# Query weights under four scales instead of one, with group 0's weight sums moved to GpSimd

## Chip, cores and metric

One NeuronCore of a Trainium2 chip runs one program. The metric is the device time of a run in microseconds. A core has a matrix engine (TensorE, PE in the profile, with its weight loads as PEld), VectorE (DVE), ScalarE (ACT), GpSimd (POOL) and a queue that issues DMAs (SyncE, SP). Each works through its own list of instructions in order, and they wait for each other by semaphores.

## The reference

Two blocks read the same normalised input, and the output joins them:

```
xn = layernorm(x)                          # 2048 x 640
q  = (xn @ wq), 32 heads of 192            # wq is 640 x 6144
p  = softmax(q k^T / sqrt(192)), the last 512 keys of the cache
s  = (p v, heads joined) @ wo              # wo is 6144 x 640
h  = sigmoid(xn @ w_gate) * (xn @ w_up)    # 2048 x 1536
g  = silu(h @ w_down)
out = x + s * g
```

All inputs and the output are bf16.

## The kernel before

**Opening** (lines 272 to 559). The 2048 rows of x stand in four tiles of 512 (s = 0 to 3). For each tile the kernel makes xn, turns it by DMA, and runs twelve steps f. A step multiplies a 128-wide slice of w_gate and of w_up (ten matmuls, L493) into a pair of PSUM banks; four pairs are used in turn. ACT takes the sigmoid (L498), and DVE multiplies the two halves into hT_sb (L499). After a tile, four DMAs (store_h, L479) write hT to DRAM (h_d); it is read again much later. Two hT buffers take turns.

Beside these steps the opening prepares the attention. It multiplies q with Strassen-like sums: a product of 2 x 2 blocks in seven half-size products, so that both xn and wq need sums and differences of their blocks in fp16. sum_x (L448) makes those of xn on DVE, six per half pi of the rows; it needs a copy of the odd tile with its partition halves exchanged, which swap (L440) makes by four DMAs on SP. Wq comes in eight groups of 768 columns (two pairs of heads each), each in five chunks c of its rows: load_raw (L223) loads a chunk, scale_raw (L238) scales it to fp16 on ACT or DVE, copy_w (L248) and sum_w (L256) write the sums.

The scale must be known first. It is a power of two near the largest sum of magnitudes, so the whole of wq is read once more: sixteen slices of 128 x 1920 (scan_load, L196) are reduced, thirteen by ACT's Abs with an accumulator (scan_abs, L295) and three by DVE (scan_fold, L200). set_scale (L208) reduces the sums to one number per partition and turns it by a DMA (mx_row); set_scale2 (L216) takes the maximum over it and writes w_up (for the weights) and w_down (for K, scale_k, L164, so that the scores come out the same). One scale serves all groups. Group 0's sums are made in the opening, by ACT (copies) and DVE (subtractions) at the steps in scale_at and sum_at; group 1's raw chunks are scaled at the steps in raw_at.

**Attention** (from L561). Sixteen runs r = (pi, g): a half of the rows and a group. Before run 0 its queries are made alone, in eleven slots (query_slots, L592; the list at L751): a slot is ten matmuls (L584) into PSUM banks, copied by `saved` (L603 on ACT) to a tile qp and added by DVE (L622) into qT. Between the slots second_w (L265) makes two chunks of group 1 on GpSimd and loads the next. In a run there are 16 score steps k (stage_s, L667: six matmuls, L678, and ACT's exponential, L682, into E; two pairs of banks in turn), with the slots for the next run's queries between them (q_after, L758), and then eight steps of p times v (stage_pv, L684: L692 on PE, L698 and L699 on DVE). phase_s (L833) hangs other work on steps k: K and V loads, sums of magnitudes over v and wo on ACT (abs_v, abs_wo). The sums of a later group's weights run at the end of a run (weights, L760) on ACT and GpSimd.

**End.** After the attention come the products with w_down and wo (L1000).

**What sets the order.** The schedule is written by hand: each engine's list has the order of the program text, and SP's and POOL's lists include their DMAs. Memory is laid out by pools. The opening's pools are closed before the attention's are opened, and those take the same addresses from the bottom up; the first instruction that writes into a reused address waits for everything that still reads or writes it. In the opening the pools stand in the order wB (w_gate, w_up, and four scan slices "more"), bwork, bone, hpool (the two hT), xpool, xin_pool, xt_pool. In the attention: arm_pool, small, qT_pool, qp_pool, e_pool, ost_pool, oT_pool. One tile, mid, serves both.

The copy out of a slot's product, and the place of the pool that the opening's hT takes:

```
            else:
                t = qp_pool.tile([P, 512], F32, name="qp")[:]
            copy(t, b, act)
            return t
...
        bone = bctx.enter_context(tc.tile_pool(name="bone", bufs=1))
        hpool = bctx.enter_context(tc.tile_pool(name="hpool", bufs=2))
        xpool = bctx.enter_context(tc.tile_pool(name="xpool", bufs=4))
```

Of the kernel before, what the change touches and what calls it, by code (L numbers as in the profile page):

```python
# [9 lines left out]
ALU = mybir.AluOpType  # L10
# [7 lines left out]
def kernel(  # L18
# [88 lines left out]
    def part(tile_, at, shape, dtype):  # L107
        n = 1
        for m in shape:
            n *= m  # L110
        v = tile_[:, at:at + n]
        if dtype != BF16:
            v = v.bitcast(dtype)
        names = "abc"[:len(shape)]
        if len(shape) == 1:
            return v
        return v.rearrange(
            f"p ({' '.join(names)}) -> p {' '.join(names)}", **{c: m for c, m in zip(names[1:], shape[1:])}
        )
# [10 lines left out]
    w_sc = const.tile([P, 17], F32, name="w_sc")  # L130
    mx_h, h_up, h_down, mx_w, wd_up, wd_down, g_scale = (w_sc[:, i:i + 1] for i in range(10, 17))
# [6 lines left out]
    mx, w_up, w_down, mx_o, o_up, o_down, mx_v, v_up, v_down, descale = (w_sc[:, i:i + 1] for i in range(10))  # L138
# [8 lines left out]
    wq_n = A_wq.rearrange("(p c) n -> p (c n)", p=P)  # L147
# [16 lines left out]
    def scale_k(key):  # L164
        k_sb = k_pool.tile([P, KC * PC, 2, HF], BF16, name="k_sb")
        for i in range(2):
            nc.vector.tensor_scalar(k_sb[:, :, i, :], kraw_of[key][:, i, :, :], w_down, None, op0=ALU.mult)
        k_of[key] = k_sb
# [21 lines left out]
    NPC = 16  # L190
    NSC = NG * NCD * GC // NPC
    assert NSC <= NW // 4
    scan_bufs = [part(mid, (2 * n + 1) * NCD * 512, (NSC,), BF16) for n in (1, 2, 3)]
    scan_bufs += [part(mid, NX + i * NW // 4, (NSC,), BF16) for i in range(4)]

    def scan_load(i, eng):  # L196
        scan_t[i] = scan_bufs[i % len(scan_bufs)]
        eng.dma_start(scan_t[i], wq_n[:, i * NSC:(i + 1) * NSC])

    def scan_fold(wm, i, first):  # L200

        v = scan_t[i]
        bits = (wm[:] if first else v).bitcast(I32)
        nc.vector.tensor_single_scalar(bits, v.bitcast(I32), 0x7FFF7FFF, op=ALU.bitwise_and)
        if not first:
            nc.vector.tensor_tensor(wm[:], wm[:], v, ALU.max)
# [9 lines left out]
    def set_scale2(mx=mx, up=w_up, down=w_down, k=1.0 / 4096):  # L216
        nc.vector.tensor_reduce(mx, mx_row[:, 0, :], axis=mybir.AxisListType.X, op=ALU.max)
        nc.vector.tensor_scalar(down, mx, k, None, op0=ALU.mult)
        nc.vector.reciprocal(up, down)  # L219
# [3 lines left out]
    def load_raw(g, c, eng):  # L223
        raw = raws[raw_next[0] % 3]
        raw_next[0] += 1
        for r in (LO, HI):
            eng.dma_start(raw[r], wq_r[:, c, :, g * GC:(g + 1) * GC])  # L227
        raw_t[g, c] = raw
# [9 lines left out]
    def scale_raw(g, c, on_act=True):  # L238
        raw = raw_t[g, c]
        if on_act:  # L240
            nc.scalar.activation(raw.bitcast(F16), raw, AF.Copy, scale=w_up)  # L241
        else:
            nc.vector.tensor_scalar(raw.bitcast(F16), raw, w_up, None, op0=ALU.mult)
# [4 lines left out]
    def copy_w(g, c, copy):  # L248
        for k, r in enumerate((LO, HI)):
            copy(sums_w(g, c, r, 0), part_w(g, c, r, k, 0))  # L250
# [13 lines left out]

    def second_w(c):  # L265

        copy_w(1, c, nc.gpsimd.tensor_copy)
        sum_w(1, c, nc.gpsimd.tensor_tensor, nc.gpsimd.tensor_copy)
        load_raw(1 + (c + 3) // NCD, (c + 3) % NCD, nc.gpsimd)


    with ExitStack() as bctx:
# [3 lines left out]
        hpool = bctx.enter_context(tc.tile_pool(name="hpool", bufs=2))  # L276
        xpool = bctx.enter_context(tc.tile_pool(name="xpool", bufs=4))
        xin_pool = bctx.enter_context(tc.tile_pool(name="xin_pool", bufs=1))
        xt_pool = bctx.enter_context(tc.tile_pool(name="xt_pool", bufs=1))

# [9 lines left out]
        wmax = bone.tile([P, NSC], BF16, name="wmax")  # L290
        scans = bone.tile([P, 14], F32, name="scans")
        scan_out = bone.tile([P, 3 * D], BF16, name="scan_out")
        x_tiles = {}

        def scan_abs(i, col):  # L295
            nc.scalar.activation(scan_t[i], scan_t[i], AF.Abs, accum_out=scans[:, col:col + 1])
# [40 lines left out]
        more = wB.tile([P, 4, NSC], BF16, name="more")  # L337
        scan_bufs.extend(more[:, i, :] for i in range(4))
        for i in range(4):
            scan_load(i, nc.sync)  # L340
# [107 lines left out]
        def sum_x(pi, k, x_sw):  # L448
# [12 lines left out]
            elif k == 5:  # L461
                tt(xb[HI], ev[HI], xb[HI], ALU.subtract)

        sums = {(1, 4): (0, 4), (1, 10): (0, 0), (1, 11): (0, 1), (2, 7): (0, 2), (2, 9): (0, 3), (2, 11): (0, 5),
                (3, 2): (1, 0), (3, 3): (1, 1), (3, 5): (1, 2), (3, 8): (1, 3), (3, 9): (1, 4), (3, 10): (1, 5)}
        folds = {(1, 7): 10, (1, 8): 11, (1, 9): 12}
        scan_act = {(0, 7): 0, (0, 8): 1, (0, 9): 2, (0, 10): 3, (1, 1): 4, (1, 2): 5, (1, 3): 6, (1, 7): 7, (1, 8): 8,
                    (1, 10): 9, (2, 0): 13, (2, 1): 14, (2, 2): 15}
        scan_loads = {(0, 8): (4, 5, 6), (0, 9): (7,), (0, 10): (8,), (0, 11): (9,), (1, 1): (10, 11, 12),
                      (1, 7): (13, 14, 15)}  # L470
        abs_at = [(0, 3), (0, 4), (2, 4), (3, 4)]
        scale_at = {(2, 7): 0, (2, 9): 1, (3, 0): 2, (3, 3): 3, (3, 6): 4}
        sum_at = {(2, 8): 0, (2, 10): 1, (3, 1): 2, (3, 4): 3, (3, 7): 4}
        raw_at = {(3, 8): 0, (3, 10): 1}
# [6 lines left out]
        for s in range(NST):  # L481
            hT_sb = hpool.tile([P, TQ, NF, P], BF16, name="hT_sb")
            pi = s // 2
            if s % 2 == 1:
                sw = swap(pi)
            for f in range(NF):
# [31 lines left out]
                if (s, f) in folds:  # L518
                    scan_fold(wmax, folds[s, f], folds[s, f] == 10)
                if (s, f) in scan_act:  # L520
                    scan_abs(scan_act[s, f], 1 + list(scan_act).index((s, f)))
# [4 lines left out]
                for i in scan_loads.get((s, f), ()):  # L526
                    scan_load(i, nc.sync)
                if (s, f) == (2, 1):
                    nc.vector.tensor_reduce(scans[:, 0:1], wmax[:], axis=mybir.AxisListType.X, op=ALU.max)
                    for c in range(3):  # L530
                        load_raw(0, c, nc.sync)
                elif (s, f) == (2, 3):
                    set_scale(scans[:])
                elif (s, f) == (2, 6):
                    set_scale2()
                if (s, f) in ((1, 1), (2, 4), (3, 1)):
                    store_h(s - 1, h_last)
                if (s, f) in scale_at:
                    scale_w(0, scale_at[s, f])
                if (s, f) in raw_at:  # L540
                    scale_raw(1, raw_at[s, f])
                if (s, f) in sum_at:
                    c = sum_at[s, f]
                    sum_w(0, c)
                    load_raw((c + 3) // NCD, (c + 3) % NCD, nc.sync if s == 2 else nc.gpsimd)
                if (s, f) == (2, 8):
                    load_k((0, 0))
                if s == 3:
                    if f in (0, 7):
                        scale_k((0, f // 7))  # L550
                    elif f in (3, 9):
                        turn_k((0, f // 9))
                    if f == 0:
                        load_k((0, 1), nc.gpsimd)
                    elif f == 6:
                        for hp in range(G):
                            load_v(0, hp, nc.sync)
# [8 lines left out]
    wo_in = [part(arm, NW + n * NWC * D, (NWC, D), BF16) for n in range(4)]  # L566
    v_abs = part(arm, NW + 2 * NO, (KC, DH), BF16), part(mid, NX, (KC, DH), BF16)
    assert 3 * NO + KC * DH <= NW + NR
# [182 lines left out]
    for n, k in enumerate((0, 1, 7, 2, 3, 8, 4, 5, 9, 6, 10)):  # L751
        slots[k]()
        if n == 1:
            nc.scalar.activation(mx, w_up, AF.Exp, scale=0.0)
        if n < 2:
            second_w(n)
    scale_s = {0: 2, 3: 3, 15: 4}
# [75 lines left out]
    def phase_s(r, pi, g, k, q_list, pv_list):  # L833
# [24 lines left out]
        if pi == 1 and g < NG - 1 and k in (1, 3, 4, 5):  # L858
            abs_v(g, (1, 3, 4, 5).index(k))
        if r in (2, 10) and k == 7:  # L860
            set_scale(*((hw_sum[:, 0:4], mx_h) if r == 2 else (hw_sum[:, 4:8], mx_w)))
# [39 lines left out]
    for r, (pi, g) in enumerate(runs):  # L901
# [23 lines left out]
        for k, (q, x) in enumerate(pv_list):  # L925
            stage_pv(q, *x)
            if r == last - 1 and k == 1:
                set_scale(v_sum[:], mx_v)
            if k in (5, 7):
                store_o(2)  # L930
            if pi == 0 and 1 <= g < 5 and k == 6:
                w = wo_in[3 * g % 4]
                nc.scalar.activation(w, w, AF.Abs, accum_out=hw_sum[:, 3 + g:4 + g])
            if pi == 0 and 1 <= g < NG - 1 and k in (2, 4):
                weights(g + 1, 2 + k // 2)
            if pi == 1 and g + 2 < NG and k in (1, 3, 5):
                weights(g + 2, k // 2)
# [254 lines left out]
```

## Time and profile before

| | |
|---|---|
| median of 3 runs | 888.09 us (887.02 to 888.36) |
| the profiled execution's own time | 887.34 us |
| its span in the profile | 885.6 us |
| mean granted clock of TensorE | 0.993 |
| busy: PE, DVE, ACT, POOL | 868.2, 679.7, 629.3, 211.8 us |
| PE busy, 14 to 116 us | 99.32 of 102 us |
| DVE and ACT busy, 14 to 116 us | 74.38 and 80.97 us |
| one run of the attention (172.4 to 205.1 us) | 32.7 us, PE busy throughout |

The span is what the hardware profiler saw of the program; the time of the execution lies 1.74 us above it. The page gives, per engine, the busy time; slices of a fortieth of the span with tenths of busy time; the clock that TensorE was granted; the chain of waits that ended last; and groups of instructions by line with their mean duration. A window's row has the busy time of each engine in it. A timeline's row has start, duration, engine, line, operation, tiles, and in brackets the idle time before it with what ended it.

### The profile page before, as it was taken

How to read it: one execution, taken by the hardware profiler on the slowest of the kernel's cores; microseconds unless marked ns; L12 is line 12 of the kernel's file. 1: busy time of each engine (PE TensorE's matmuls, PEld its weight loads, DVE VectorE, ACT ScalarE, POOL GpSimd, SP SyncE). 2: the span in 40 equal slices, each digit the busy share in tenths (PEclk: the TensorE clock that was granted, in tenths of full speed). 3: DMA queues.
4: the chain of work that ended last, by engine and by line, in shares of the span. 5: the costliest groups of instructions: out<-in, count | busy, mean ns of one | idle time of the engine just before them, and what ended most of it. 6: DMA issues, size and time to landing. Idle time of an engine off the chain costs nothing.

```text
span 885.6 us, 19009 instructions
## 1 busy us (share of the span) xinstructions
PE 868.2 (98%) x7548; PEld 568.9 (64%) x7557; DVE 679.7 (77%) x1153; ACT 629.3 (71%) x784; POOL 211.8 (24%) x293
## 2 busy tenths in 40 slices
PE   9999959999999999999999999999999999999998
PEld 5444425756766765765775775775777777777775
DVE  6587757777777777777777877787888788879997
ACT  6867746488888888888888786747555666866662
POOL 0000175206415415425424423300000110000000
PEclk9999979999999999999999999999999999999999
DMA  9997881689789789799779769799695976776741
GB/s 279 270 292 159 237 197 37 95 228 211 151 218 213 154 217 219 137 214 236 127 196 225 140 153 203 187 224 259 138 286 176 304 238 208 236 267 212 220 141 38
DMA packets 257177, 175.88 MB, mean 199 GB/s; under 512 B 162432, under 2 KB 239872, under 8 KB 257088
## 3 DMA queue, kind: packets, MB, share of 16 engines
q1 hardware_dynamic: 251040, 155.59, 68.7%
q0 software_dynamic: 6048, 19.08, 10.9%
q8 instruction: 59, 0.97, 0.5%
q14 instruction: 30, 0.25, 0.1%
HBM read 101.71 MB, written 36.70 MB: 156 GB/s over the span
## 4 chain that ended last, share of the span: by engine, by line
PE 84%; issue 1%; DVE 1%; ACT 0%; ACTq 0%; DVEq 0%
PE ps_all L1000 25%; PE ps_all L584 20%; PE ps_all L692 20%; PE ps_all L678 19%; DVE arm L984 0%; DVE arm L1055 0%; DVE arm L1053 0%; DVE qT L622 0%; ACT qp L603 0%; ACTq L603 0%; DVEq L622 0%; DVEq L1053 0%
## 5 line engine op out<-in xcount | busy, mean ns | idle before, releaser
L682 ACT ACTIVATE E<-ps_all 128x1024 bf16<-128x1024 f32 x256 | 251.2, 1022 | 113.5 <-PE ps_all L678 112.8
L678 PE MATMUL ps_all<-qT,kT 64*128 64x512 bf16 x1536 | 198.1, 376 | 0.0
L692 PEld LDWEIGHTS <-E 128*128 128x128 bf16 x2048 | 169.7, 98 | 8.1 <-issue 8.1
L692 PE MATMUL ps_all<-v_sb,E 128*128 128x193 bf16 x2048 | 174.0, 247 | 0.0
L622 DVE TENSOR_TENSOR qT<-ps_all,qp 128x512 bf16<-128x512 f32 x174 | 115.5, 687 | 54.5 <-PE ps_all L584 36.8
L1000 PEld LDWEIGHTS <-mid 128*128 128x128 f16 x1236 | 120.3, 98 | 46.0
L605 DVE COPY qp<-ps_all 128x512 f32<-128x512 f32 x150 | 100.5, 687 | 46.5 <-PE ps_all L584 46.5
L678 PEld LDWEIGHTS <-kT 64*128 64x128 bf16 x1536 | 84.9, 94 | 79.4 <-issue 4.4
L699 DVE TENSOR_TENSOR o_st<-ps_all,rden 128x768 bf16<-128x768 f32 x128 | 122.5, 957 | 4.6 <-DVE rden L698 0.2
L584 PE MATMUL ps_all<-mid 64*128 64x512 f16 (+1 forms) x840 | 109.8, 383 | 8.9 <-ACT qp L603 4.5
L584 PE MATMUL ps_all<-mid,arm 64*128 64x512 f16 (+1 forms) x840 | 105.6, 376 | 0.0
L584 PEld LDWEIGHTS <-mid 64*128 64x128 f16 x840 | 49.9, 95 | 55.3 <-issue 15.2
L584 PEld LDWEIGHTS <-arm 64*128 64x128 f16 x840 | 47.1, 94 | 44.6 <-issue 0.2
L1000 PE MATMUL ps_all<-arm,mid 128*128 128x320 f16 x480 | 70.4, 299 | 0.0
L813 ACT ACTIVATE mid<-mid,w_sc 128x1536 f16<-128x1536 bf16 (+1 forms) x43 | 61.4, 1451 | 0.0
L241 ACT ACTIVATE mid<-mid,w_sc 128x1536 f16<-128x1536 bf16 x37 | 58.2, 1572 | 2.5 <-DVE w_sc L219 1.9
L1000 PE MATMUL ps_all<-op,mid 128*128 128x320 f16 (+1 forms) x408 | 58.1, 295 | 0.0
L499 DVE TENSOR_TENSOR hT_sb<-ps_all,sig_sb 128x512 bf16<-128x512 f32 x48 | 32.8, 684 | 26.3 <-ACT sig_sb L498 17.0
L1000 PE MATMUL ps_all<-mid 128*128 128x320 f16 x348 | 49.9, 299 | 0.0
L259 POOL TENSOR_TENSOR arm<-mid 128x384 f16<-128x384 f16 x20 | 19.3, 963 | 114.5 <-ACT mid L241 113.5
L227 POOL DMA_DIRECT2D mid<-in_A_wq_dram x70 | 41.7, 598 | 13.4 <-DVE mid L263 13.4
L698 DVE RECIPROCAL rden<-ps_all 128x4 f32<-128x4 f32 x128 | 23.3, 182 | 27.7 <-PE ps_all L692 26.1
(189 smaller groups left out, 1055.6 us busy)
## 6 DMA issues: line engine op xcount, KB each, us to landing
oT_d<-oT SPq DMA_DIRECT2D x64, 384.0 KB, 5.5
mid<-oT_d SPq DMA_DIRECT2D x46, 384.0 KB, 4.1
mid<-in_A_wq_dram POOLq DMA_DIRECT2D x70, 192.0 KB, 6.5
arm<-in_A_wo_dram SPq DMA_DIRECT2D x16, 480.0 KB, 5.8
h_d<-hT_sb SPq DMA_DIRECT2D x16, 384.0 KB, 5.7
v_sb<-in_A_v_cache_dram SPq DMA_DIRECT2D x32, 192.0 KB, 6.1
mid<-in_A_wq_dram SPq DMA_DIRECT2D x12, 480.0 KB, 7.4
kraw<-in_A_k_cache_dram SPq DMA_DIRECT2D x30, 192.0 KB, 3.2
```

Source lines behind the costliest of these rows:

```text
L227: eng.dma_start(raw[r], wq_r[:, c, :, g * GC:(g + 1) * GC])
L241: nc.scalar.activation(raw.bitcast(F16), raw, AF.Copy, scale=w_up)
L499: nc.vector.tensor_tensor(hT_sb[:, :, f, :], *(v.rearrange("p (q n) -> p q n", q=TQ) for v in (gu[:, 1, :], sig_sb[:])), ALU.mult,)
L584: nc.tensor.matmul(ps_all[:, b, :], lhsT=w(r, c), rhs=x[r, c, :], start=(first and k == 0), stop=(k == len(cs) - 1), skip_group_check=True,)
L605: nc.vector.tensor_copy(dst, part(b))
L622: nc.vector.tensor_tensor(q_out(i, u, pp), part(b), t, ALU.add)
L678: nc.tensor.matmul(ps[:, b, :], lhsT=kT[h, c * PC + j, :], rhs=qT_t[r][i, j][h, pp, :], start=(j == 0), stop=(j == PC - 1),)
L682: nc.scalar.activation(E_t[r, i, pp][:, c, :, :], ps, AF.Exp, scale=scale_qk)
L692: nc.tensor.matmul(o_ps[:, q // 2, q % 2, 0:DH + 1], lhsT=E[:, c, h, q * P:(q + 1) * P], rhs=vt[:, c, 0:DH + 1], start=(c == 0), stop=(c = ...
L699: nc.vector.tensor_tensor(o_st[:, :, h * DH:(h + 1) * DH].rearrange("p (b i) d -> p b i d", b=2), o_ps[:, :, :, 0:DH], rden[:].to_broadcas ...
L813: eng.activation(t, t.bitcast(BF16), AF.Copy, scale=up)
L1000: nc.tensor.matmul(ps_all[:, b, d0:d1], lhsT=a[:, c, :], rhs=w[:, c, d0:d1], start=(start and c == 0), stop=(c == nk - 1), skip_group_chec ...
```

## The change

**Scales.** wq is scanned in twenty slices of 128 x 1536 instead of sixteen of 128 x 1920: five slices (one per c) for each set of two groups. There are four sets, each with a pair of w_ups and w_downs. Set 0 is scanned in the opening, by ACT alone, at steps 7 to 11 of tile 0; its scale is set at steps (1, 0) and (1, 2). Sets 1 to 3 are scanned by ACT in the attention: slices 5 to 9 after run 0's scores, 10 and 11 among run 0's scores (k = 4 and 10), 12 to 19 one per run at the end of runs 1 to 8. Their scales are set in runs 1, 4 and 9, with the same operations and one more mx_row DMA each. Six slices are loaded by SP between the slots before run 0, the others a run ahead. DVE's three folds and its reduce are gone.

**Group 0's sums.** pool_w makes copies and subtractions of a chunk on GpSimd, where ACT and DVE did; chunks 0 to 4 of group 0 are scaled by ACT at the steps (1, 3), (1, 7), (1, 10), (2, 2), (2, 8), and two of group 1 at (3, 1), (3, 4). All raw loads of the opening go over SP, and so do those of K for pair (0, 1).

**Buffers.** hpool moves behind xt_pool; "more" and the 3840-byte wmax are gone. In the built program the tiles that matter lie at these byte addresses of a partition:

| | before | after |
|---|---|---|
| hT_sb, two | 74848 to 99424 | 91520 to 116096 |
| x_odd, two, and x_sw | 114784 to 135264 | 71040 to 91520 |
| qp, four | 76288 to 84480 | 76384 to 84576 |
| E, four | 84480 to 117248 | 84576 to 117344 |

**Steps.** Some of sum_x, abs_up and store_h stand at other steps. TensorE's instructions are the same in number and order.

The diff, cut to its core:

```diff
-        hpool = bctx.enter_context(tc.tile_pool(name="hpool", bufs=2))
         xpool = bctx.enter_context(tc.tile_pool(name="xpool", bufs=4))
         xin_pool = bctx.enter_context(tc.tile_pool(name="xin_pool", bufs=1))
         xt_pool = bctx.enter_context(tc.tile_pool(name="xt_pool", bufs=1))
+        hpool = bctx.enter_context(tc.tile_pool(name="hpool", bufs=2))
...
+    NSC = 2 * GC
+    NPC = NSET * NCD
+    def scan_load(i, buf):
+        scan_t[i] = buf[:, 0:NSC]
+        n, c = divmod(i, NCD)
+        nc.sync.dma_start(scan_t[i], wq_n[:, c, n * NSC:(n + 1) * NSC])
+    def scan_abs(i):
+        nc.scalar.activation(scan_t[i], scan_t[i], AF.Abs, accum_out=scan_sum[:, i:i + 1])
+    def set_scan(n):
+        set_scale(scan_sum[:, n * NCD:(n + 1) * NCD])
...
+    def pool_w(g, c):
+        copy_w(g, c, nc.gpsimd.tensor_copy)
+        sum_w(g, c, nc.gpsimd.tensor_tensor, nc.gpsimd.tensor_copy)
...
-        more = wB.tile([P, 4, NSC], BF16, name="more")
-        scan_bufs.extend(more[:, i, :] for i in range(4))
-        for i in range(4):
-            scan_load(i, nc.sync)
+        for i, x in enumerate((XA[1], XB[1], XC[1], x_even[1], x_odds[1])):
+            x = x.rearrange("p c n -> p (c n)")
+            scan_load(i, x if x.dtype == BF16 else x.bitcast(BF16))
...
-        sums = {(1, 4): (0, 4), (1, 10): (0, 0), (1, 11): (0, 1), (2, 7): (0, 2), (2, 9): (0, 3), (2, 11): (0, 5),
-                (3, 2): (1, 0), (3, 3): (1, 1), (3, 5): (1, 2), (3, 8): (1, 3), (3, 9): (1, 4), (3, 10): (1, 5)}
-        folds = {(1, 7): 10, (1, 8): 11, (1, 9): 12}
-        abs_at = [(0, 3), (0, 4), (2, 4), (3, 4)]
-        scale_at = {(2, 7): 0, (2, 9): 1, (3, 0): 2, (3, 3): 3, (3, 6): 4}
-        sum_at = {(2, 8): 0, (2, 10): 1, (3, 1): 2, (3, 4): 3, (3, 7): 4}
-        raw_at = {(3, 8): 0, (3, 10): 1}
+        sums = {(1, 4): (0, 4), (1, 9): (0, 0), (1, 11): (0, 1), (2, 7): (0, 2), (2, 9): (0, 3), (2, 11): (0, 5),
+                (3, 2): (1, 0), (3, 3): (1, 1), (3, 5): (1, 2), (3, 7): (1, 3), (3, 8): (1, 4), (3, 10): (1, 5)}
+        abs_at = [(1, 8), (2, 9), (3, 2), (3, 6)]
+        raw_loads = {(0, 9): (0, 0), (0, 10): (0, 1), (0, 11): (0, 2), (1, 11): (0, 3), (2, 3): (0, 4),
+                     (2, 9): (1, 0), (2, 11): (1, 1), (3, 5): (1, 2)}
+        raw_at = {(1, 3): (0, 0), (1, 7): (0, 1), (1, 10): (0, 2), (2, 2): (0, 3), (2, 8): (0, 4),
+                  (3, 1): (1, 0), (3, 4): (1, 1)}
...
+                if s == 0 and 7 <= f:
+                    scan_abs(f - 7)
+                if (s, f) in raw_loads:
+                    load_raw(*raw_loads[s, f], nc.sync)
+                if (s, f) == (1, 0):
+                    set_scan(0)
+                    sw = swap(0)
+                elif (s, f) == (1, 2):
+                    set_scale2()
+                if (s, f) in raw_at:
+                    scale_raw(*raw_at[s, f])
+                    if raw_at[s, f][0] == 0:
+                        pool_w(*raw_at[s, f])
...
         if n < 2:
             second_w(n)
+        elif n == 4:
+            for i in range(6):
+                scan_load(NCD + i, scan_bufs[i])
+    scans_s = {(0, 4): 10, (0, 10): 11}
+    scans_pv = {(0, 0): 5, (0, 1): 6, (0, 2): 7, (0, 4): 8, (0, 6): 9, (1, 7): 12, (2, 7): 13, (3, 7): 14}
+    scans_pv.update({(4 + n, 7): 15 + n for n in range(NCD)})
+    scans_load = {(0, 6): (11, 5), (1, 4): (12, 4), (2, 4): (13, 5), (3, 4): (14, 4)}
+    scans_load.update({(4 + n, 4): (15 + n, 5 - n % 2) for n in range(NCD)})
+    sets = {(1, 1): 1, (4, 1): 2, (9, 1): 3}
+    sets2 = {(1, 8): 1, (4, 9): 2, (9, 8): 3}
```

## The prediction

> **What bounds the kernel now.** I read the page first. TensorE (PE) is busy for almost the whole span, so time can only go where it is not; the slices show one such place.
>
> ```profile
> PE 868.2 (98%) x7548; PEld 568.9 (64%) x7557; DVE 679.7 (77%) x1153; ACT 629.3 (71%) x784; POOL 211.8 (24%) x293
> ...
> PE   9999959999999999999999999999999999999998
> ...
> PEclk9999979999999999999999999999999999999999
> ```
>
> Slice 6 (110.7 to 132.8 us) is half empty and its granted clock is 0.7. Next I asked for busy times by window around it:
>
> ```profile
> 96.00:116.00 20.00, 18.06 (x81) 7.82 (x81) 15.73 (x29) 15.23 (x22) 4.77 (x8) 1.00 1.07 265
> 116.00:120.00 4.00, 2.89 (x20) 1.08 (x20) 3.94 (x5) 3.51 (x5) 3.20 (x3) 1.00 1.02 197
> 120.00:125.00 5.00, 2.22 (x9) 0.65 (x9) 2.67 (x3) 0.00 (x0) 4.70 (x5) 0.77 0.28 112
> 125.00:130.00 5.00, 0.53 (x2) 0.10 (x1) 0.41 (x1) 1.08 (x2) 4.67 (x8) 0.50 1.01 296
> 130.00:135.00 5.00, 4.80 (x33) 2.14 (x33) 1.56 (x3) 4.32 (x8) 3.05 (x5) 0.71 0.63 142
> 135.00:150.00 15.00, 15.00 (x141) 8.76 (x139) 12.14 (x20) 8.82 (x12) 7.69 (x12) 1.00 0.10 27
> ```
>
> The columns are the window, its length, then busy time of PE, PEld, DVE, ACT, POOL, then clock, DMA share, GB/s. PE is idle 1.94 us before 116 and about 8.6 us from 116 to 135. In windows of 20 us from 135 to 875 PE is busy all the time: later work has no hole to fill and must only not make one. The timeline says who is late at the join of opening and attention:
>
> ```profile
> 122.04 0.69 DVE L499 TENSOR_TENSOR hT_sb<-ps_all,sig_sb 128x512 bf16<-128x512 f32 x1
> 122.76 2.32 SPq L479 DMA_DIRECT2D h_d<-hT_sb  x4
> 122.78 2.29 PE L584 MATMUL ps_all<-mid 64*128 64x512 bf16 x9 [2.85 <-DVE hT_sb L499]
> ...
> 128.90 1.08 ACT L603 ACTIVATE qp<-ps_all 128x512 f32<-128x512 f32 x2 [9.39 <-issue]
> 129.55 0.58 PE L584 MATMUL ps_all<-mid 64*128 64x512 f16 x1 [4.47 <-ACT qp L603]
> ```
>
> PE finishes the opening's last matmul at 115.3, but DVE makes the last hT only by 122.73: its queue is backed up with sums. Four stores of that hT to DRAM follow. ACT's first copy out of the query products (qp) waits 9.39 us; the timeline calls it "issue", but the view of the tile h_d names this copy as its one waiter, 9.4 us. In the built program qp lies over an hT buffer. The chain of waits, in order of time, agrees:
>
> ```profile
> 119.51 9.23 issue
> ...
> 130.33 9.58 PE ps_all L584 x74
> 139.91 1.29 PE ps_all L678 x12
> 141.20 1.08 PE ps_all L584 x10
> ```
>
> The first score matmul starts at 139.91, that is 24.67 us after the first query matmul (115.24). One query slot (10 matmuls) takes 1.08 us when nothing waits.
>
> **The change, part by part.**
>
> *Order of buffers.* In the built program of the changed kernel qp lies over x_odd and x_sw, hT only under the E tiles. ACT's first qp copy then waits for the four swap DMAs of the fourth tile, long landed, and for its product. The h_d wait moves to the first exponential.
>
> *Sums of group 0 on GpSimd.* DVE loses five chunks of four subtractions (0.35 + 0.36 + 0.36 + 0.36 = 1.43 us), three folds (0.65 + 1.16 us, the first 0.65) and a reduce of 2.10 us: 7.2 + 4.3 + 2.1 = 13.6 us. ACT loses 15 copies (0.52 us each, 7.8 us). I recount DVE's last steps with T the end of the opening's matmuls and 2.16 us per step f (ten matmuls 0.216 us apart). f7: hT 0.69, sum 1.49, K scaling 0.87 end at T-5.3. f8: hT and sum end at T-3.1. f9: hT at T-2.4. f10: hT and sum at T+0.3. f11: last hT at T+1.0, where it was T+7.4. Its PSUM bank is first needed by the third query slot, at T+2.2, so all three stalls on L499 (0.52, 0.90, 2.85 us) go.
>
> *The join anew.* Eleven slots at 1.08 us are 11.9 us. What is late next: ACT holds a table load (1.28 us) and 0.6 us copies, and its last copy before the third s3 slot ends near T+8.6, when PE is at T+8.6. DVE's additions for the last slot end near T+10.9, PE wants them at T+10.8. So 12.4 us, of 24.67: I take 12.2 us gained. The ends: 11.9 us (12.8 gained), and the eight later slots' own rate in this run, 9.58 / 8 x 11 = 13.2 us (11.5 gained); this row is partly under a clock of 0.71, and gaps up to 0.93 us at 106.85 left it at 1.00, so I lean to the first.
>
> *Opening.* PE idles 102 - 99.32 = 2.68 us between 14 and 116. The largest part, around 104 to 109, comes after DVE waited 1.67 us for x_sw, whose swap (SP, 94.52) stood behind a weight load that waited for DVE's L263. That load now waits for GpSimd, done earlier, so the swap starts near 90. Gain 0 to 2.7 us; I take 1.5. The first slice scan shrinks: 5 x 1.48 us on ACT in the opening for 13 x 1.81 us (1.48 us is interpolated from 128x768, 0.82 us start to start, and 128x1920, 1.81 us). POOL takes five chunks of some 5.5 us (126.49 to 132.0), or 8.6 beside busy DVE (116.66 to 125.25); the last starts near 82 and is wanted at T+3, so it is hidden by 20 us. Two new waits stand in queues. SP's loads of raw weights wait for GpSimd; the last ahead of the swap needs chunk 3, done by 78, and the swap is ready near 90. DVE's set_scale2 comes two steps (4.3 us) after the transpose that it reads, whose landing took 2.2 to 5.2 us: DVE may wait some 1 us near 43, and the hT behind it has three steps, 6.5 us, before PE wants its bank. I cost both at nothing.
> A row that speaks against this part: POOL's L259 and L260 took 2.02 and 2.04 us beside DVE's L460 and L462, for 0.91 alone, and L460 took 1.62 for 1.48. By the rows DVE pays 0.14 us for each of 12 sums, 1.7 us, inside its slack. The Trainium skill ("SBUF — State Buffer", section "SBUF: two separate sides") says why: the two engines share a port pair under an exclusive lock, held for an instruction. By its rule each of 12 DVE sums could wait out a GpSimd operation of 0.91 us, 10.9 us in all; the rows show the loss on POOL's side. DVE is idle 102 - 74.4 = 27.6 us there and 13.6 us are freed, so both fit; it is a rival below.
>
> *Fifteen scans in the attention.* 15 x 1.48 = 22.2 us on ACT, beside PE's work. Five follow run 0's exponentials: 7.4 us inside ACT's idle 10.55 us. Eight of the rest stand at the end of a run's PV part:
>
> ```profile
> 205.95 1.94 ACT L682 ACTIVATE E<-ps_all 128x1024 bf16<-128x1024 f32 x2 [2.54 <-PE ps_all L678]
> ```
>
> ACT is idle 2.54 us there (3.32 us at 238.79, after the next run), so 1.48 us fits. Scan 10 (k=4 of run 0) pushes exponential 5 by 0.8 us, and the pause before score 7 takes it up. Scan 11 (k=10) stands where ACT has none: exponentials 11 and 12 start at 157.44 right behind a qp copy. Moved by 1.48 us, 12 ends at 160.9, and score 14, which needs its banks, would have started at 159.44: 1.4 us lost. Bounds 0 (if exponential 11 slips ahead of need) and 3.3 us (if its load, issued behind scan 10's end, takes the longest h_d landing of 9.8 us).
>
> *Three more scales.* Each puts four DVE operations (219.33 to 220.02, 0.69 us) at k=1 and three (81.41 to 82.08) later. DVE idles 0.24 to 0.44 us per slot and catches up in two; I take 0, bound 3 x 0.69 = 2.1 us. Loads of 0.39 MB a run go over SP where nothing urgent follows.
>
> **Sum**, against this execution's own 887.34 us (span 885.6): -12.2 - 1.5 + 1.4 = -12.3, so 875.0. The median of the runs shown, 888.09, lies 0.75 above it: **875.8 us**. Ends: -12.8 - 2.7 = -15.5 (872.6) and -11.5 + 3.3 + 2.1 = -6.1 (882.0).
>
> **Rivals.**
> 1. *The store wait only moves to the first exponential.* It is wanted at T+13.1; the stores leave at T+1.0 and took 6.0 us (122.76 to 128.74). Against: 6 us of room. For: six scan slices (2.4 MB) come behind them, another h_d issue row lasted 6.17 us, and the longest landing was 9.8: 1.0 + 6.2 + 9.8 = T+17.0, 3.9 us lost: 879.7. Chance 0.18.
> 2. *GpSimd holds DVE up in the opening* (the lock above): then 1.5 us is not won and as much as today's 2.7 us comes on top: 880.0. Against: 41 us of DVE slack. Chance 0.05.
> 3. *ACT becomes the bound, slower.* If each scan delays the exponentials by its full length and PE waits, 22.2 us are paid for 13.7 won: 896.6. It decides where ACT's idle time at a run's end is under 1.48 us; the rows say 2.54. Chance 0.05.
> 4. *The join does not shorten*, because some other buffer or weight of the attention lands when hT did (weights of group 1, K): 888. Against: GpSimd's second group starts with the last hT and is first needed a run later. Chance 0.03.
> 5. *More than forecast*, under 872.6: 0.05.
>
> The forecast has 0.64. The range **872 to 882** takes in rivals 1 and 2. A run of this kernel tells 0.2% (1.8 us) from no change: faster 0.92, same 0.03, slower 0.05.
>
> **What would show it.** Right: first score matmul near 126; no idle ACT before the first qp copy over 1 us; clock 1.00 in every window from 116 to 135; last hT within 2 us of the last opening matmul; PE idle of about 1.4 us in run 0, before score 13 or 14, nowhere later. Wrong: the first exponential waiting on h_d; exponentials late at a run's start; PE idle after 160.

## The result, and the profile after

The changed kernel takes 877.85 us (median of 4 runs, 877.32 to 878.37), the kernel before beside it 887.56 us (886.62 to 888.36). The ratio is 0.9891, with a 95% interval of 0.9874 to 0.9908. The profiled execution's span is 876.1 us, where it was 885.6. The forecast was 875.8, so the direction and the place were right, and 2 us are missing.

First the page of the kernel after: busy times, then slices of PE and of its clock.

```profile
PE 865.4 (99%) x7557; PEld 570.9 (65%) x7557; DVE 674.9 (77%) x1148; ACT 628.5 (72%) x783; POOL 234.8 (27%) x320
...
PE   9999999999998999999999999999999999999998
...
PEclk9999999999999999999999999999999999999999
```

The half-empty slice 6 has gone, and with it the dip of the clock. A smaller dent has appeared at slice 13 (262.8 to 284.7 us). The windows at the join (window, length, busy PE, PEld, DVE, ACT, POOL, then clock, DMA share, GB/s):

```profile
120.00:125.00 5.00, 5.00 (x48) 2.35 (x46) 4.67 (x8) 2.22 (x5) 4.52 (x7) 1.00 1.01 330
125.00:130.00 5.00, 5.00 (x50) 2.62 (x46) 4.11 (x6) 3.82 (x4) 4.73 (x7) 1.00 1.04 251
130.00:135.00 5.00, 5.00 (x49) 2.64 (x47) 4.60 (x7) 4.29 (x5) 4.68 (x8) 1.00 0.30 61
```

PE is busy throughout and the clock is 1.00, where it was busy 2.22, 0.53 and 4.80 us at 0.77, 0.50 and 0.71. The timeline of the kernel after says why:

```profile
112.63 0.69 DVE L490 TENSOR_TENSOR hT_sb<-ps_all,sig_sb 128x512 bf16<-128x512 f32 x1
...
113.66 0.60 ACT L588 ACTIVATE qp<-ps_all 128x512 f32<-128x512 f32 x1 [1.66 <-PE ps_all L569]
...
124.83 1.94 ACT L667 ACTIVATE E<-ps_all 128x1024 bf16<-128x1024 f32 x2 [0.25 <-PE ps_all L663]
```

The last hT ends 0.9 us after the opening's last matmul (T = 112.44; for the profiles of before, T is the start of the first query matmul, which lies within 0.1 us of it). The first copy to qp waits for PE alone. The first exponential, which now lies behind the stores of hT, waits 0.25 us, for its own matmuls. The chain of waits (start, us, what; in order of time) gives the join and what follows:

```profile
112.44 11.70 PE ps_all L569 x105
124.14 1.29 PE ps_all L663 x12
...
141.72 1.46 ACT arm L202 x2
143.18 1.84 ACT E L667 x2
```

The join takes 11.70 us, which was 24.67. The first score comes at 124.14, 15.77 us earlier than before. Of that, run 0 gives back 1.22 us: scan 11 (L202) stands in the chain ahead of two exponentials. Run by run the first scores then keep a distance of 14.6 us to those of before until run 4. That run lasts 38.14 us, where it lasted 32.85, and 9.4 us are left to the end. The timeline of run 4 in the kernel after (SPq is what SP issues; the brackets hold the idle time before a row and what ended it):

```profile
259.24 5.81 SPq L690 DMA_TRANSPOSE oT<-o_st  x1
260.54 0.61 DVE L212 CAST mx_b<-w_sc 128x128 bf16<-128x128 f32 x1
...
265.78 3.44 SPq L184 DMA_DIRECT2D v_sb<-in_A_v_cache_dram  x4
...
272.27 1.31 SPq L213 DMA_TRANSPOSE mx_row<-mx_b  x1
276.58 0.29 DVE L216 TENSOR_REDUCE w_sc<-mx_row 128x1 f32<-128x128 bf16 x1 [4.43 <-DMA mx_row<-mx_b]
277.90 1.26 PE L569 MATMUL ps_all<-mid 64*128 64x512 f16 x10 [3.49 <-DVE qp L590]
```

This is the third set's scale. Its input is ready at 261.15, but SP sends the transpose only at 272.27, behind a transpose of outputs, their stores and the v loads. It lands at 276.57. DVE has reached set_scale2 4.43 us earlier and waits there, with the copies of the query products behind it; PE waits 3.49 us for those. The windows around it:

```profile
275.00:280.00 5.00, 2.10 (x16) 1.05 (x17) 1.95 (x6) 0.74 (x1) 0.00 (x0) 0.91 0.58 157
280.00:285.00 5.00, 5.00 (x39) 3.00 (x36) 2.68 (x6) 3.59 (x4) 0.00 (x0) 0.75 0.24 79
```

Around the pause the granted clock is 0.91 and 0.75, so that 3.49 us without work cost 5.29 us.

### The profile page after: what moved, and what is told of

It is laid out like the page before. It is cut to its first block, busy times and chain, and to the rows that moved or that the text cites. A ratio compares the mean times of both kernels' runs of the same rounds, so it can differ in the third digit from the quotient of the medians.

```text
span 876.1 us, 19052 instructions
## 1 busy us (share of the span) xinstructions
PE 865.4 (99%) x7557; PEld 570.9 (65%) x7557; DVE 674.9 (77%) x1148; ACT 628.5 (72%) x783; POOL 234.8 (27%) x320
## 4 chain that ended last, share of the span: by engine, by line
PE 94%; ACT 2%; DMA 1%; DVE 1%; SPq 1%; issue 0%; DVEq 0%; ACTq 0%
PE ps_all L1007 25%; PE ps_all L677 20%; PE ps_all L569 19%; PE ps_all L663 18%; PE ps_all L484 11%; ACT E L667 1%; PE ps_all L387 1%; ACT arm L722 1%; DMA mx_row<-mx_b 0%; DMA kraw<-in_A_k_cache_dram 0%; SPq L697 0%; DMA x_sb<-in_A_x_dram 0%; DVE arm L991 0%; DVE arm L1062 0%; DVE arm L1060 0%
## 5 line engine op out<-in xcount | busy, mean ns | idle before, releaser
L569 PE MATMUL ps_all<-mid 64*128 64x512 f16 (+1 forms) x840 | 106.8, 377 | 3.5 <-DVE qp L590 3.5
L490 DVE TENSOR_TENSOR hT_sb<-ps_all,sig_sb 128x512 bf16<-128x512 f32 x48 | 32.8, 686 | 28.3 <-PE ps_all L484 20.7
L489 ACT ACTIVATE sig_sb<-ps_all 128x512 bf16<-128x512 f32 x48 | 28.4, 596 | 35.3 <-PE ps_all L484 33.9
L258 POOL TENSOR_TENSOR mid<-mid 128x384 f16<-128x384 f16 x20 | 18.2, 909 | 118.9 <-ACT mid L240 117.9
```

The lines of the kernel that those rows point to most:

```text
L258: tt(TB, part_w(g, c, a, 1, 1), part_w(g, c, a, 0, 1), ALU.subtract)
L569: nc.tensor.matmul(ps_all[:, b, :], lhsT=w(r, c), rhs=x[r, c, :], start=(first and k == 0), stop=(k == len(cs) - 1), skip_group_check=True,)
```

## Experiments

The theory after this reading has four parts. The join was two waits in a row, DVE's lateness and the stores under qp, and each half of the change removes one. The opening gained because the last tile's swap goes out earlier. Scan 11 costs 1.2 us. The third set costs 5.3 us because its transpose stands behind other work on SP. The rivals are named with each run. Every time is a median; ratios are to the kernel before, run beside it (medians 887.5 to 888.3 us).

### The join: order of buffers alone, and all but the order

In the kernel before, only the pool was moved:

```diff
-        hpool = bctx.enter_context(tc.tile_pool(name="hpool", bufs=2))
         xpool = bctx.enter_context(tc.tile_pool(name="xpool", bufs=4))
         xin_pool = bctx.enter_context(tc.tile_pool(name="xin_pool", bufs=1))
         xt_pool = bctx.enter_context(tc.tile_pool(name="xt_pool", bufs=1))
+        hpool = bctx.enter_context(tc.tile_pool(name="hpool", bufs=2))
```

> The kernel before, with only the pool of hT moved behind xt_pool: DVE is as late as before (last hT 7.4 us after the opening's last matmul, T), but the first copy to qp no longer waits for the stores of hT. Theory (two waits stand one behind the other, and each part of the change removes one): third slot waits for DVE until about T+8; the second of the two spare copies, whose tile now lies under the last hT, waits for the stores until about T+13.5; four or five slots are left then; first score near T+19 instead of T+24.7, so 5 to 6 us less than before: about 882. Rival a (the stores' wait was the whole join): first score near T+13, 12 us less, about 876. Rival b (DVE's lateness was the whole): no difference, 887.6.

880.87 us, ratio 0.993 (0.9905 to 0.9954). The opening ends at 113.25 in this profile, and the first score comes at 132.78, T+19.5. The timeline of this kernel:

```profile
120.04 0.69 DVE L499 TENSOR_TENSOR hT_sb<-ps_all,sig_sb 128x512 bf16<-128x512 f32 x1
...
120.79 10.53 PE L584 MATMUL ps_all<-mid 64*128 64x512 bf16 x72 [2.84 <-DVE hT_sb L499]
```

DVE is as late as expected, at T+7.5 (120.73), and PE waits for it as before. After that PE does not stop again, so the wait that I expected at the spare copies is not there. The rest is the clock: the chain's 84 matmuls, which take 9.1 us at 0.108 us each, take 11.99, at a clock of 0.50 in the window from 120 to 125. Of the 7.2 us between this span (878.4) and that of before (885.6), 5.1 lie in the join, as the theory said; 2.0 lie in the opening, which ended earlier here.

The reverse, in the changed kernel with the pool put back behind bone:

> The changed kernel, with the pool of hT back behind bone, so that qp lies over the last hT again: DVE is on time (last hT at T+0.9), but the first copy to qp waits for the stores of hT, which leave at T+1 and took some 6 us. Theory: that copy starts near T+7 instead of T+1.2 and PE, two slots ahead, loses 5 to 6 us: first score near T+17.3, about 883.5. Rival a (order is all of the join): 12 us lost, 890. Rival b (order is nothing once DVE is on time): 877.9.

884.32 us, ratio 0.9961 (0.9948 to 0.9974), where 883.5 was expected. DVE is on time (last hT at T+1.0, with T = 112.50), and ACT's first copy waits:

```profile
118.96 1.08 ACT L588 ACTIVATE qp<-ps_all 128x512 f32<-128x512 f32 x2 [6.84 <-DMA h_d<-hT_sb]
```

Here the row itself names the stores, where it said "issue" in the kernel before. The first score comes at 131.07, T+18.6. So the join is 24.67 us with both waits, 19.5 without the stores' wait, 18.6 with DVE on time, and 11.70 with neither. Both rivals, that one wait alone is the join, fall.

### The opening

The changed kernel with group 0's sums given back to ACT and DVE, at the same early steps:

```diff
                     if raw_at[s, f][0] == 0:
-                        pool_w(*raw_at[s, f])
+                        copy_w(*raw_at[s, f], copy_act)
+                        sum_w(*raw_at[s, f])
```

> The changed kernel, with the sums of group 0 made as before by ACT (three copies of 0.52 us a chunk) and DVE (1.43 us a chunk), at the steps where it gives them to GpSimd, (1, 3) to (2, 8). Theory a (the end of the opening is freed because those sums no longer stand in its last tile, whoever makes them): DVE and ACT have the room between 42 and 90 us, the last hT comes again within 2 us of the last opening matmul, 877.9 within 1 us. Theory b (GpSimd's taking them over is what counts): DVE falls behind by some of its 7.2 us and the opening or the join gets 2 to 5 us longer, 880 to 883.

877.44 us, ratio 0.9879 (0.9857 to 0.9902), the same as the changed kernel. The opening ends at 112.53, the last hT at 113.41, the join takes 11.70 us. Theory a holds: GpSimd is not what counts. What is left is where the sums stand: at the steps (1, 3) to (2, 8) and no longer in the last tile, up to (3, 7), where DVE has the swap's sums to do. Those steps are open because the first set's scale is known early: ACT scales the first chunk at 43.62 us in the changed kernel and at 82.1 in the kernel before. That the steps are the cause, and not two sums of x that stand a step earlier or the folds that DVE no longer has, is argued; no run sets them apart.

The changed kernel with the last swap sent later:

```diff
-            if s == 3:
-                sw = swap(pi)
...
+                if (s, f) == (3, 2):
+                    sw = swap(1)
```

> The changed kernel, with the last tile's swap moved on SP behind the loads of K and the stores of hT of the tile before, so that its four DMAs go out near 96 as in the kernel before, instead of 86 to 90. Theory (the opening of the kernel before lost its 2 to 2.8 us because this swap came late and DVE, waiting for x_sw, made hT late): DVE waits 6 to 8 us at the first sum of the last tile, PE runs out of PSUM banks some 4 steps later and loses 1 to 3 us ahead of 112; the last hT comes later than T+1 and the join loses up to 3 more: 879 to 883. Rival (the loss came from the sums and folds that DVE no longer has, not from the swap): DVE's room takes the wait up, the opening ends within 0.5 us of 112.4 and the time is 877.9.

881.25 us, ratio 0.9922 (0.9899 to 0.9944). Its timeline and window:

```profile
99.99 1.48 DVE L447 TENSOR_TENSOR mid<-x_odd,mid 64x2560 f16<-64x2560 bf16 x1 [5.95 <-DMA mid<-x_odd]
...
107.32 1.85 PE L482 MATMUL ps_all<-x_odd,wu_sb 128*128 128x512 bf16 x5 [2.21 <-DVE hT_sb L488]
```

```profile
104.00:112.00 8.00, 5.79 (x20) 2.18 (x18) 6.48 (x7) 3.95 (x6) 0.00 (x0) 0.79 0.96 189
```

DVE waits for the swap 5.95 us and once more 2.98 us. PE waits 2.21 us, then runs at a lower clock, and the opening ends at 116.72, 4.28 us later. That is more than the 1 to 3 us that I gave it. The join stays at 11.70 us: the last hT is ready at T+2.0, still in time. So a late swap does cost the opening time, but it is not what made the last hT late in the kernel before.

The kernel before, profiled once more:

> The kernel before, unchanged, profiled once more: how far its opening and its join repeat. Theory (its opening loses 2.7 us to PE waiting at the same places every time): opening's last matmul ends again near 115.2, first score near 139.9, join 24.7 us. Rival (the opening's waits differ from execution to execution, as the order-only kernel's 113.3 suggests): the opening ends between 113 and 115.5 while the join keeps 24.7 us within 0.5.

One time, 886.99 us. The opening ends at 114.69 (115.24 in the first profile, 113.25 with the order alone), and the join takes 24.87 us. Two executions of the kernel before thus differ by 0.55 us. The 2 us appear only against the order alone, whose instructions up to there are the same but for addresses; whether that is chance is not shown. Eight profiles with the new steps end the opening between 112.2 and 112.6.

Where the old opening waits, rows of its first profile show:

```profile
104.58 1.49 DVE L454 TENSOR_TENSOR mid<-x_odd,x_sw 64x2560 f16<-64x2560 bf16 x1 [1.67 <-DMA x_sw<-x_odd]
...
106.85 1.24 PE L493 MATMUL ps_all<-x_odd,wu_sb 128*128 128x512 bf16 x5 [0.93 <-DVE hT_sb L499]
...
107.49 0.52 ACT L246 ACTIVATE mid<-mid 64x384 f16<-64x384 f16 x1 [1.55 <-DVE mid L260]
...
108.68 1.24 PE L493 MATMUL ps_all<-x_odd,wg_sb 128*128 128x512 bf16 x5 [0.59 <-ACT sig_sb L498]
```

DVE waits for the swap, and its hT comes late. Then ACT's copy of group 0 waits for DVE's subtraction, and the sigmoid behind it comes late too. PE's two waits make 1.52 us here, 1.66 in the second profile and 0.74 with the order alone, where DVE waits 1.75 us for the swap as well; the changed kernel has neither. So the swap is one part of the loss, and the sums of group 0, which ACT and DVE hand to each other, are another. From 14 to 116 us ACT waits 7.2 us for those subtractions in the kernel before, and 1.9 us in the kernel that makes the same sums at the early steps.

### Scan 11 and the third set of scales

```diff
-    scans_s = {(0, 4): 10, (0, 10): 11}
-    scans_pv = {(0, 0): 5, (0, 1): 6, (0, 2): 7, (0, 4): 8, (0, 6): 9, (1, 7): 12, (2, 7): 13, (3, 7): 14}
+    scans_s = {(0, 4): 10}
+    scans_pv = {(0, 0): 5, (0, 1): 6, (0, 2): 7, (0, 4): 8, (0, 6): 9, (0, 7): 11, (1, 7): 12, (2, 7): 13, (3, 7): 14}
```

> The changed kernel, with scan 11 moved from among run 0's scores (k = 10) to the PV part of run 0 (step 7). Theory: run 0 lasts 33.8 us instead of 32.6 because this scan of 1.5 us stands between two exponentials where ACT has no room; moved, run 0 lasts 32.6: 1.2 us less, about 876.6, with run 4 as long as before (38.1 us). Rival (PE's loss in run 0 comes from the slow start of the exponentials in the new join): run 0 stays at 33.8 us, 877.9.

876.79 us, ratio 0.9881 (0.9858 to 0.9904). Run 0 lasts 32.57 us (124.35 to 156.92), which was 33.79; run 4 still lasts 37.27. That is as expected. The times alone (875.88 to 878.20, against 877.32 to 878.37) would not show it; the length of run 0 does.

```diff
-    sets2 = {(1, 8): 1, (4, 9): 2, (9, 8): 3}
+    sets2 = {(1, 8): 1, (5, 0): 2, (9, 8): 3}
```

> The changed kernel, with the second half of the third set of scales (the three operations on DVE that read mx_row) moved from step 9 of run 4 to step 0 of run 5. The transpose that brings mx_row stays where it is and goes out as late as before, near 272. Theory: run 4 lasts 38.1 us because DVE waits 4.4 us for that transpose with the qp copies of the queries behind it, and nothing else; without the wait it lasts 32.8 us as its neighbours do: 5.3 us less, 872.6. Rival (run 4 is long because of SP's held-up loads or ACT's sums, and the wait is only their sign): run 4 keeps 36 us or more, 876 to 878.

872.77 us, ratio 0.9834 (0.9815 to 0.9854), where 872.6 was expected. SP sends the transpose late again (269.94), nobody waits for it, and run 4 lasts 32.76 us. So the wait is the loss. Why the transpose is late, two runs asked. The first sent it from ACT's queue:

```diff
-        set_scale(scan_sum[:, n * NCD:(n + 1) * NCD])
+        set_scale(scan_sum[:, n * NCD:(n + 1) * NCD], eng=nc.scalar if n == 2 else nc.sync)
...
-        nc.sync.dma_start_transpose(mx_row[:], mx_b[:])
+        eng.dma_start_transpose(mx_row[:], mx_b[:])
```

> The changed kernel, with the transpose of the third set's scale (run 4, step 1) issued from ACT's queue instead of SP's. Theory (the transpose is late because it stands on SP behind two transposes of outputs and the v loads that wait): it goes out right after its input, near 261, lands by 266, DVE does not wait at step 9; ACT may stand up to 1.5 us for the input, behind it an exponential: run 4 lasts 32.8 to 34 us, 872.6 to 874. Rival (the transpose itself or the place of the maximum is late, whichever queue issues it): DVE waits as before and run 4 keeps 37 us or more, 877 to 878.

883.04 us, ratio 0.9955 (0.9939 to 0.9971): 5.2 us slower than the changed kernel, and neither side's number. ACT's rows in run 4:

```profile
270.90 1.24 ACTq L213 DMA_TRANSPOSE mx_row<-mx_b  x1
272.19 1.94 ACT L667 ACTIVATE E<-ps_all 128x1024 bf16<-128x1024 f32 x2 [11.86 <-DMA v_sb<-in_A_v_cache_dram]
```

The transpose leaves no earlier, and ACT stands 11.86 us in front of it; run 4 lasts 46.32 us. The row puts the wait down to a landing of the v loads, which this transpose does not read. SP's stores of transposed outputs go out at 270.48, ACT's transpose at 270.90; that fits a wait until SP's transposes have landed, but no row shows it. So this run does not tell SP's order from a wait for the earlier transposes. The Trainium skill, "DMA: Bandwidth & Descriptors", section "Silent corruption: two transposing streams in flight at once", says that a second queue's transpose must wait for the first queue's to complete; if the program keeps to that rule, the 11.86 us are its price here.

The second put the v loads behind the transpose, on SP:

```diff
             set_scan(sets[r, k])
+            if r == 4:
+                for pp in range(G):
+                    load_v(g, pp, nc.sync)
...
-        if pi == 1 and g + 1 < NG:
+        if pi == 1 and g + 1 < NG and r != 3:
             for pp in range(G):
                 load_v(g + 1, pp, nc.sync)
```

> The changed kernel, with run 4's four v loads put behind the transpose of the third set's scale on SP instead of ahead of it; both halves of the set stay at steps 1 and 9. After the run with ACT's queue, two theories of the late transpose are left. Theory a (SP works in order, and what stands ahead of the transpose makes it late): the four loads took SP 3.4 us; without them the transpose goes out near 268.8 instead of 272.3, DVE waits about 1 us instead of 4.4, PE 0 to 1 us instead of 3.5: run 4 lasts 32.8 to 34 us, 873 to 874.5. Theory b (the transpose waits for the transposes of outputs before it to land, whatever stands between): it goes out at 272 again, run 4 keeps 38.1 us, 877.9.

874.15 us, ratio 0.9845 (0.9831 to 0.986). SP and DVE in run 4:

```profile
266.88 1.64 SPq L213 DMA_TRANSPOSE mx_row<-mx_b  x1
...
272.96 0.29 DVE L216 TENSOR_REDUCE w_sc<-mx_row 128x1 f32<-128x128 bf16 x1 [0.69 <-DMA mx_row<-mx_b]
```

The transpose goes out 5.4 us earlier, DVE waits 0.69 us, PE not at all, and run 4 lasts 32.80 us. Theory a holds: SP's own order, with the v loads in it, made the transpose late. Not all of the 5.4 us is the order: the four loads take SP 3.4 us, and with the order unchanged the transpose went out at 269.94 in the run that moved the second half. This kernel's 874.15 lies above the 872.77 of that run; in its profile run 6 lasts 33.82 us: there DVE waits 1.20 us for a K load that stands behind v loads on SP in the same way.

### Both repairs

The changed kernel with scan 11 at (0, 7) of the PV part and the third set's second half at step 0 of run 5:

> The changed kernel with both moves: the second half of the third set of scales at step 0 of run 5, and scan 11 in the PV part of run 0. Theory: the two losses are apart in time and add up, run 0 and run 4 both last 32.6 to 32.8 us: 5.1 and 1.1 us less than the changed kernel's 877.9 us, so 871.7. Rival (ACT or DVE, now without a pause, run into each other later): 872.5 or more, with a run over 33.5 us somewhere.

871.37 us (871.29 to 871.70), ratio 0.982 (0.9805 to 0.9835), where 871.7 was expected: the fastest version, 6.5 us under the changed kernel. The first score comes at 124.03, run 0 lasts 32.57 us, and none of runs 1 to 13 lasts over 32.90.

## Why the prediction was right, and where it was wrong

- **The bound.** The join was the hole, and the changed kernel fills it: right.
- **Join, 12.2 us gained.** It gained 24.67 - 11.70 = 12.97 us, just past the upper end (12.8). The eleven slots took 11.70 us, less than the 11.9 taken for slots alone, so ACT's table load and copies (0.5 us taken) delayed nothing. The order of the two waits was right; the runs with one of them each left 19.5 and 18.6 us. ACT was idle 1.66 us before the first copy, over the 1 us that I named as a sign, but for PE's product and not for the stores. What I did not price apart is the clock: after PE stood, matmuls ran at a clock of 0.50 for 5 to 6 us in both, so a wait costs more than its length.
- **Opening, 1.5 us gained.** Measured 2.8 us against the first profile of before, 2.2 against the second: the size was low, by the second profile inside the bound of 2.7, by the first just past it. The mechanism that I named, the swap behind a weight load, is supported by the run with a late swap, but it is one part only: PE's second wait, 0.59 us, came from ACT standing behind DVE's subtractions. How much of the 2.8 us is chance in the old opening stays open, as the profile with the order alone ended it at 113.25.
- **GpSimd.** I took the relief of DVE by 13.6 us as the cause of DVE being on time. The run without GpSimd gives 7.2 us of that back to DVE and loses nothing, so the engine is not the cause; the earlier steps, which the early scale opens, are what remains. The reading of DVE, "its queue is backed up with sums", also left out ACT, whose copies wait for DVE's subtractions while DVE waits for the sigmoids behind them. The effect was right, its reason only half.
- **Two new waits in the opening** at no cost: right. DVE found mx_row landed at 42.97, without a wait, and the swap went out from 86.38, ahead of the 90 that I had expected.
- **Scan 11, 1.4 us lost.** Measured 1.22, at the place that was named: PE stands 0.80 us right before score 13.
- **Three more scales, "I take 0, bound 3 x 0.69 = 2.1 us".** This is the step that failed, and its sign, "PE idle after 160", came: 3.49 us before 277.90. It counted DVE's instructions and not the transpose between the two halves. Sets 1 and 3 cost nothing, set 2 cost 5.29 us, outside the bound. "Loads of 0.39 MB a run go over SP where nothing urgent follows" was said of the loads; the transpose itself is urgent, and what stands ahead of it on SP was not listed. Between the halves of set 2 lie 11.0 us of DVE (261.15 to 272.15), enough for a landing of 4.3 us; but the transpose went out 16.2 us after its run's start in run 4, and 6.1 us after it in run 1.
- **Sum.** -12.97 - 2.8 + 1.22 + 5.29 = -9.3 us in place of -12.3; the span moved by 9.5. The gains were 2.1 us larger than forecast, and the loss that was missed is 5.3 us. That the total still lies 2 us from the forecast is in part luck: one error hides some of the other.
- **Rivals.** The store wait at the first exponential did not come (0.25 us, for PE). ACT did not become the bound: the scans at the ends of runs cost nothing. The lock between GpSimd and DVE is there, at the size below, and the opening did not feel it.

## What to carry to other kernels

When a step is split into two halves with a DMA between them, read the list of the queue that sends this DMA, from the moment its input is ready to the moment its output is wanted, and add up what stands ahead, waits included; the engine's own instructions are the small part. Where a join is late, list its waits in the order in which they end and expect each repair alone to stop at the next one. And before work is moved to another engine, try moving it to another step: here the engine was not what counted.

## What the runs showed of the hardware that was not expected

- **A pause of PE costs one and a half to two times its length.** In the kernel with the late swap, 2.21 us of waiting were followed by 35 matmuls in 9.40 us (7.56 at 0.216 each), at a clock of 0.79 over 104 to 112; 3.49 us made run 4 5.29 us longer. The Trainium skill, "TensorE: Matmul & The Clock Gate", section "Why this matters for your kernels", advises against gaps over some 3 us; here 2.21 us were enough.
- **DVE and GpSimd slow each other by fractions of an instruction.** The same sum beside GpSimd's work (kernel after) and without it (the kernel without GpSimd's sums):

```profile
47.43 2.21 DVE L455 TENSOR_TENSOR mid<-mid,x_odd 64x2560 f16<-64x2560 bf16 x1
```

```profile
49.17 1.48 DVE L455 TENSOR_TENSOR mid<-mid,x_odd 64x2560 f16<-64x2560 bf16 x1
```

Five sums of the opening met GpSimd's operations. Four took 2.21, 2.00, 1.81 and 1.84 us, 1.9 us more together than in the other kernel, and one, which met the end of an operation, 1.50; I had estimated 1.7 for twelve. On the other side a GpSimd operation of 0.91 us took 2.04 three times. The loss falls on whichever comes second, which agrees with the exclusive lock that the Trainium skill states ("SBUF — State Buffer", section "SBUF: two separate sides").
- **One run's length can wander where it hangs on a queue.** Run 4 with the wait in it lasted 35.6, 37.3, 37.9, 38.1 and 39.0 us in five profiles; without it 32.8.
